# RetNet recurrence and a tanh-shrink layer on one core: a rewritten order of the first eight steps, and the last rows stored in four pieces

## The chip, the core and the metric

The kernel runs on one core of one Trainium2 chip. The metric is device time in microseconds (us), lower is better. A core has TensorE (PE: matrix products, result in PSUM), VectorE (DVE), ScalarE (ACT) and GpSimd (POOL), which each work through their own instructions in order, and SyncE (SP), which here only issues DMAs. They wait for each other through semaphores.

## What is computed

```python
# q, k, v: (4, 8, 768, 64) float32; w_in (512, 2048), w_out (2048, 512) float64
gamma = 1.0 - 2.0 ** (-5.0 - np.arange(H))
for t in range(S):
    state = gamma * state + k_t (outer) v_t        # per batch and head
    y[:, :, t] = (1 / sqrt(D)) * q_t @ state
x = y as (B*S, H*D) = (3072, 512)
h = x @ w_in
out = (h - tanh(h)) @ w_out                        # (3072, 512) float32
```

## The kernel before, in words

The recurrence is done in 24 chunks of 128 tokens (six per batch, `CPB`). A chunk's `q` and `v` are scaled by powers of gamma (`scale`, L241), `k` and `q` are transposed on TensorE (`turn`, L255) and copied to SBUF by ScalarE (`turn_copy`, L267, L269); `products` (L303, L309) makes k-by-v and k-by-q products, `mask` (L316) and `state` (L326 to L332) work on them on VectorE, and `outputs`, `outputs_rest` (L357) accumulate y in PSUM. Between these two, `see` (L387) reads four columns of y. `keep_x` (L402) copies y out as x, transposed.

The layer is done in tiles of 256 tokens (`n`) by 256 hidden columns (`m2`), called steps. `up` (L421) makes h in two halves, `shrink_begin` to `shrink_end` (ScalarE L431 to L449, VectorE L459 to L482) make g = h - tanh(h), `down` (L490) multiplies with w_out and `add_up` (L503) adds up in SBUF. Later steps use a scheme with seven products instead of eight for a pair of 2x2 blocks (`fast_up` L735, `fast_products` L627).

The weights come as float64 and are turned into float32 in the kernel, in blocks of 128 rows or columns: `load_weights` (L154, L159) fetches the raw words, `convert_begin` (ScalarE, L177, L178), `convert_bits` (VectorE, L186 to L192) and `convert_end` (L200, L204, VectorE or GpSimd) build the numbers.

What bears on the order: the program runs with a hand-written schedule (`tc.manual_schedule()`), so each engine and each DMA queue does things in the order in which the Python code names them. For the first eight steps (`BEGUN = 8`) and the first eight chunks that order is a string of pieces, each a letter and a number. The letters: `L` load a chunk's k, q, v; `W` load a weight block; `s`, `w` scale q, v; `t`, `T` transpose k, q; `c`, `C` copy these; `p` products; `m` mask; `z` state; `b`, `r` first and second part of the outputs; `e` see; `y` keep x; `A`, `D`, `G` the three parts of a conversion; `u`, `v` the two halves of an up; `a`, `q`, `d`, `g` the shrink; `o` down; `E` add up; and `x`, which sets how many matmuls on a tile of zeros (`keep_busy`, L217) are put ahead of the next piece of TensorE, in the PSUM place which that piece will write. The numbers count chunks, weight blocks or steps. After this string a loop over the remaining steps sets the order.

Some buffers tie engines together: k and q have two buffers each (`inp`), so chunk c+2 is fetched when the products of chunk c are done; the transposes from chunk 4 on and the products share one pair of PSUM banks (tag `t`); the h banks are two; the last chunks' y share two banks.

At the end (`finish`) the last down products come in four groups, and a chain of additions builds the four quarters c11, c12, c21, c22 of the last 256 rows. `late_c22` copies a PSUM bank on ScalarE (L658) and adds on GpSimd (L659); `store` (L647) writes one of two halves of the rows, 256 KB each.

Of the kernel before, what the change touches and what calls it, by code (L numbers as in the profile page):

```python
# [16 lines left out]
P = 128  # L17
# [7 lines left out]
B0, C0 = 1.1162213056058772, 5.494931718829769  # L25
B1, C1 = -1.609711559785289, 5.546157850574988
# [6 lines left out]
def kernel(  # L33
# [25 lines left out]
    nc = tc.nc  # L59
# [12 lines left out]
    TH = 2 * P  # L72
# [15 lines left out]
    def bank(tag, name):  # L88
        return ps.tile([P, BANK], F32, tag=tag, name=name)
# [25 lines left out]
    w1 = wts.tile([P, NC, DF], F32, name="w1")  # L115
    w2 = wts.tile([P, NM, DM], F32, name="w2")
# [6 lines left out]
    def weight_ends(i):  # L123


        f, r = divmod(i, 2 * NC)
        if r < NC:
            cols = ts(NC * f + r, P)
            rows = w_in[:, cols].rearrange("(k two p) n -> p two k n", two=2, p=P)

            return w1[:, :, cols], [
                (ds(0, P), 0, rows[:, 0]),
                (ds(0, D), 1, rows[D:, 1]),
                (ds(D, D), 1, rows[:D, 1]),
            ]
        m = NC * f + r - NC
        return w2[:, m], w_out[ts(m, P)]
# [57 lines left out]
    def convert_end(i, engine):  # L195
        if i not in words:
            return
        dst, src = weight_ends(i)
        head, low, power = words.pop(i)
        engine.tensor_tensor(low, low, power.bitcast(F32), op=ALU.mult)  # L200
        head = head.bitcast(F32)
        if isinstance(src, list):
            low, head = (t.rearrange("p (c n) -> p c n", c=NC) for t in (low, head))
        engine.tensor_tensor(dst, low, head, op=ALU.add)  # L204
# [10 lines left out]
    def keep_busy(at):  # L215
        for _ in range(idle[0]):
            nc.tensor.matmul(at, busy, busy, start=True, stop=True, skip_group_check=True)  # L217
        idle[0] = 0
# [18 lines left out]
    def scale(ci, which, engine):  # L237
        if ci >= NCH:
            return
        t, g = loaded[ci][1 + which], (gq, gv)[which]  # L240
        engine.tensor_tensor(t, t, g[:, ts(ci % CPB, H)][:, :, None].to_broadcast([P, H, D]),  # L241
                             op=ALU.mult)
# [47 lines left out]
    scores = {}  # L290
# [28 lines left out]
        masked[ci] = m  # L319

    def state(ci):
        halves = scores.pop(ci)
        j = ci % CPB
        if j == 0:
            states[ci] = mid.tile([P, 2, NP, D], F32, tag="state", name=f"state_{ci}", bufs=3)
            nc.vector.tensor_copy(states[ci][:, 1], halves[:, 0, 1])  # L326
        else:
            nc.vector.tensor_tensor(states[ci][:, 1], halves[:, 0, 1], states[ci][:, 0],
                                    op=ALU.add)
        if j < CPB - 1:  # L330
            nxt = mid.tile([P, 2, NP, D], F32, tag="state", name=f"state_{ci + 1}", bufs=3)
            nc.vector.tensor_tensor(nxt[:, 0], halves[:, 1, 1], states[ci][:, 1], op=ALU.add)  # L332
            states[ci + 1] = nxt
# [75 lines left out]
    hps = {}  # L409

    def work(tag, bufs):
        return tmp.tile([P, BANK], F32, tag=tag, name=tag, bufs=bufs)

    def up(n, m2, i):

        if i == 0:
            hps[n, m2] = bank("h", f"h_{n}_{m2}")
        hp = hps[n, m2][:, ts(i, TH)]
        keep_busy(hp[:, :P])
        for c in range(NC):  # L420
            nc.tensor.matmul(hp, w1[:, c, ts(2 * m2 + i, P)], xT[n // 2][:, c, ts(n % 2, TH)],  # L421
                             start=(i == 0 and c == 0), stop=(c == NC - 1),
                             skip_group_check=True)
# [69 lines left out]
    def add_up(n, m2, j):  # L493
        done = 2 * m2 + 2 == NM
        if j == 0 and n not in sums:
            sums[n] = [op.tile([P, 2, DM], F32, tag="sum", name=f"sum_{n}"), set()]
        o, begun = sums[n][0][:, j], sums[n][1]
        if j in begun:
            nc.vector.tensor_tensor(o, o_p[j], o, op=ALU.add)
        elif done and j % 2:  # L500
            nc.vector.tensor_copy(o, o_p[j])
        else:
            nc.scalar.copy(out=o, in_=o_p[j])  # L503
        begun.add(j)
        if done:
            nc.sync.dma_start(out=rows_of(n)[:, j], in_=o)

    def rows_of(n):

        return out[ds(n * TH, TH)].rearrange("(p two) c -> p two c", two=2)  # L510
# [13 lines left out]
    steps = [(n, m2, i == 0, i == len(r) - 1) for r in runs for i, (n, m2) in enumerate(r)]  # L524
# [107 lines left out]
    def sums_of(n):  # L632

        acc = accs[n]
        o = op.tile([P, 2, DM], F32, tag="sum", name=f"sum_{n}")
        c11, c12, c21, c22 = (o[:, j, ts(c, TH)] for j in range(2) for c in range(2))
        some = [mid.tile([P, 2, TH], F32, tag="a", name=f"fast_{n}") for _ in range(2)]
        p1, v_, x_, w_ = (t[:, i] for t in some for i in range(2))

        def add(dst, k, b, sub=False):  # L640
            if sub:
                nc.vector.tensor_tensor(dst, b, acc[k], op=ALU.subtract)
            else:
                nc.vector.tensor_tensor(dst, acc[k], b, op=ALU.add)

        def store(j, queue=nc.sync):
            queue.dma_start(out=rows_of(n)[:, j], in_=o[:, j])  # L647

        todo = {
            "p1": lambda: nc.scalar.copy(out=p1, in_=acc[1]), "c11": lambda: add(c11, 2, p1),  # L650
            "v": lambda: add(v_, 6, p1), "w": lambda: add(w_, 7, v_),
            "c22": lambda: add(c22, 5, w_), "x": lambda: add(x_, 5, v_),
            "c21": lambda: add(c21, 4, w_, True), "c12": lambda: add(c12, 3, x_),
        }

        def late_c22():
            p5 = work("q0", 1)[:, :TH]
            nc.scalar.copy(out=p5, in_=acc[5])  # L658
            nc.gpsimd.tensor_tensor(c22, p5, w_, op=ALU.add)  # L659

        return todo, store, late_c22
# [14 lines left out]
    def finish(n, m2, first, last):  # L676

        todo, store, late_c22 = None, None, None
        for some, then in (((1, 2), ("p1", "c11")), ((6,), ("v",)), ((7, 5), ("w", "x")),
                           ((4, 3), ("c21", "c12"))):  # L680
            fast_products(n, m2, first, last, some)
            if todo is None:
                todo, store, late_c22 = sums_of(n)
            for x in then:
                todo[x]()
                if x == "w":
                    late_c22()
                if x == "c21":
                    store(1, nc.scalar)
        store(0)  # L690

    def end_some(n):
        for _ in range(min(n, len(ending))):
# [85 lines left out]

    BEGUN = 8  # L780
    EARLY_TURNS = 4
    TO_VECTOR = 2

    def tall(ci):
        return nc.vector if ci < TO_VECTOR else nc.gpsimd

    pieces = {
        "L": load_chunk,
        "W": load_weights,
        "s": lambda c: scale(c, 0, tall(c)),  # L790
        "w": lambda c: scale(c, 1, tall(c)),
        "t": lambda c: turn(c, 0, c < EARLY_TURNS),
        "T": lambda c: turn(c, 1, c < EARLY_TURNS),
        "c": lambda c: turn_copy(c, 0),
        "C": lambda c: turn_copy(c, 1 if c < EARLY_TURNS else None),
        "p": products,
        "m": mask,
        "z": state,
        "b": outputs,
        "e": see,  # L800
# [1 line left out]
        "y": keep_x,  # L802
        "A": convert_begin,
        "D": convert_bits,
        "G": lambda i: convert_end(i, tall(i)),
        "u": lambda s: up(*steps[s][:2], 0),
        "v": lambda s: up(*steps[s][:2], 1),
        "a": lambda s: shrink_begin(*steps[s][:2]),
# [2 lines left out]
        "g": lambda s: [f(*steps[s][:2]) for f in (shrink_last_factor, shrink_end)],  # L811
        "o": lambda s: [down(*steps[s][:2], j, *steps[s][2:]) for j in range(2)],
        "E": lambda s: [add_up(*steps[s][:2], j) for j in range(2)],
        "x": lambda n: idle.__setitem__(0, n),
    }
    if w_out.dtype != F32:
        rooms += [xp.tile([P, 2, 2 * BANK], U32, tag="xT", name=f"raws_{i}") for i in range(3)]
    order = """
    L0 x8 t0 c0 s0 x5 T0 w0 L1 C0 x3 t1 W0 p0 c1 s1 m0 x2 T1 z0 W1 C1 w1 x3 b0 p1 e0 A0 r0
    m1 z1 y0 A1 D0 L2 x4 b1 t2 e1 c2 G0 r1 s2 y1 D1 x3 T2 w2 L3 u0 C2 W2 p2 G1 s3 t3 m2 T3  # L820
    w3 c3 v0 z2 C3 b2 A2 L4 p3 e2 W3 D2 a0 r2 s4 y2 w4 q0 W4 m3 z3 G2 x9 t4 b3 A3 d0 T4 e3
    C4 r3 g0 L5 y3 x1 p4 A4 W5 u2 D3 s5 v2 W6 w5 m4 D4 u1 G3 a2 q2 z4 L6 x6 t5 d2 G4 T5 A5
    v1 W7 C5 g2 b4 s6 a1 W8 p5 w6 e4 u3 D5 q1 v3 m5 A6 G5 z5 r4 L7 a3 t6 d1 b5 W9 y4 T6 e5
    o0 s7 g1 C6 w7 A7 W10 D6 q3 r5 t7 W11 T7 D7 G6 y5 C7 x3 u4 d3 v4 G7 A8 g3 p6 a4 o1 A9 m6
    z6 q4 D8 p7 E1 d4 G8 b6 o2 e6 m7 g4 A10 r6 z7 u5 y6 D9 b7 v5 D10 G9 e7 r7 a5 o3 y7 q5
    G10 u6 E3 d5 A11 v6 g5 o4 a6 D11 q6 u7 G11 d6 v7 g6 o5 a7 q7 E5 d7 g7 W12 L8 W13 W14
    """
    for piece in order.split():
        pieces[piece[0]](int(piece[1:]))
# [65 lines left out]
    for s in range(BEGUN, len(steps)):  # L895
        n, m2, first, last = steps[s]
        fast = n >= FAST_UP
        ci = with_chunk.get(s)
# [115 lines left out]
```

## Time and profile before

| what | value |
|---|---|
| median of 7 runs (lowest, highest) | 712.98 us (711.7, 714.05) |
| the profiled execution's own time | 711.87 us |
| its span, first to last instruction | 710.0 us |
| TensorE busy | 698.5 us (98%), zero-tile matmuls included |
| VectorE, ScalarE, GpSimd busy | 576.6, 432.2, 348.1 us |
| DMA | 59.95 MB, mean 84 GB/s |
| zero-tile matmuls ahead of pieces (`x`) | 47, each shown as two records |

A page of the profile gives busy times, the span in 40 equal slices, the chain of work that ended last, the costliest groups and the DMA issues. Other views answer questions: a timeline lists instructions in order of time (start in us, duration in us, engine, line, operation, tiles, shape, count, and in brackets the idle time of that engine before it and what ended it); a table of stages gives each engine's busy time between two times; a list of waits gives who waited for whom. A TensorE float32 matmul appears as two records. In the timeline the duration of the last matmul of a group overlaps the next group by its pipeline depth, so the spacing of starts is what counts.

### The profile page before, as it was taken

What the parts mean: (1) busy time and instruction counts of PE and PEld (TensorE: products, weight loads), DVE (VectorE), ACT (ScalarE), POOL (GpSimd) and SP (SyncE); (2) the same over time, 40 slices, a digit from 0 to 9 for tenths busy, and PEclk for the clock granted to TensorE, in tenths of its full rate; (3) what the DMA queues carried; (4) which work ended last, traced back from release to release, by engine and by line L of the source; (5) the groups of instructions that cost most, each with busy time, mean ns of one, the idle gap of its engine ahead of it and who ended that gap; (6) DMA issues with size and microseconds to landing.
All of it is one profiled execution on the core that took longest, in us unless ns stands there. A gap on an engine that the chain in (4) does not pass through costs nothing.

```text
span 710.0 us, 16725 instructions
## 1 busy us (share of the span) xinstructions
PE 698.5 (98%) x6574; PEld 573.5 (81%) x6574; DVE 576.6 (81%) x976; ACT 432.2 (61%) x814; POOL 348.1 (49%) x493
## 2 busy tenths in 40 slices
PE   8899999999999999999999999999999999999997
PEld 8686666667666776676779999999999999999996
DVE  4999988898899866688687888788787787887885
ACT  4567565777676755566575556666555555665553
POOL 0574436445444582565378854454353544543333
PEclk9999999999999999999999999999999999999999
DMA  9974428966966466555200000000000000000001
GB/s 202 220 198 106 105 61 205 217 172 165 200 186 165 110 161 164 133 150 128 69 32 1 1 2 16 16 1 31 1 1 31 0 1 30 2 16 16 2 16 45
DMA packets 125406, 59.95 MB, mean 84 GB/s; under 512 B 109840, under 2 KB 118160, under 8 KB 125328
## 3 DMA queue, kind: packets, MB, share of 16 engines
q1 hardware_dynamic: 122736, 50.08, 29.6%
q10 hardware_dynamic: 2592, 8.80, 3.2%
q8 instruction: 52, 0.85, 0.5%
q14 instruction: 26, 0.21, 0.1%
HBM read 35.80 MB, written 14.68 MB: 71 GB/s over the span
## 4 chain that ended last, share of the span: by engine, by line
PE 92%; DVE 4%; DMA 1%; ACT 1%; SPq 0%; issue 0%; DVEq 0%; ACTq 0%
PE h L735 28%; PE o L490 18%; PE h L421 15%; PE fast_t L627 9%; PE y L627 8%; PE fast_o L627 7%; PE y L357 3%; PE s L309 1%; PE s L303 1%; PE kqTp L217 1%; PE kqTp L255 1%; DMA raw<-in_moe_w_in_dram 1%; DMA kqT<-rows 1%; DVE head L190 1%; DVE power L192 0%
## 5 line engine op out<-in xcount | busy, mean ns | idle before, releaser
L490 PE MATMUL o<-w,g 128*128 128x512 f32 x320 | 145.9, 594 | 0.0
L434 ACT ACTIVATE th<-h 128x512 f32<-128x512 f32 x64 | 38.2, 597 | 138.8 <-DVE h L752 136.3
L421 PE MATMUL h<-xT,w 128*128 128x256 f32 x512 | 117.8, 382 | 1.4 <-DVE w L204 1.4
L421 PEld LDWEIGHTS h<-xT,w 128*128 128x128 f32 x512 | 95.7, 190 | 21.5 <-issue 7.4
L578 POOL TENSOR_TENSOR s<-g 128x128 f32<-128x128 f32 x56 | 25.6, 457 | 165.3 <-DVE g L482 147.6
L490 PEld LDWEIGHTS o<-w,g 128*128 128x128 f32 x320 | 58.8, 190 | 54.3 <-issue 52.1
L200 POOL TENSOR_TENSOR low<-low,power 128x512 f32<-128x512 f32 x30 | 38.6, 1288 | 102.4 <-DVE power L192 66.5
L735 PEld LDWEIGHTS h<-xT,w 128*128 128x128 f32 x512 | 76.2, 191 | 14.5 <-issue 6.9
L482 DVE COPY_PREDICATED g<-large,th 128x512 f32<-128x512 int32 x96 | 76.7, 799 | 9.8 <-DVE g L481 0.5
L735 PE MATMUL h<-xT,w 128*128 128x128 f32 x512 | 78.7, 276 | 0.2 <-ACT fast_head L740 0.2
L459 DVE TENSOR_TENSOR th<-h,th 128x512 f32<-128x512 f32 x96 | 65.5, 682 | 15.2 <-ACT th L432 13.9
L465 DVE SCALAR_TENSOR_TENSOR h<-q,h 128x512 f32<-128x512 f32 x96 | 66.8, 696 | 11.4 <-ACT q L440 1.5
L750 DVE TENSOR_TENSOR h<-h,fast_head 128x256 f32<-128x256 f32 x64 | 27.6, 432 | 53.8 <-PE h L735 52.0
L440 ACT ACTIVATE q<-u,tab 128x512 f32<-128x512 f32 x96 | 69.7, 726 | 1.7
L448 ACT ACTIVATE q<-u,tab 128x512 f32<-128x512 f32 x96 | 69.5, 723 | 0.0
L745 POOL TENSOR_TENSOR fast_head<-fast_head 128x256 f32<-128x256 f32 x64 | 47.2, 738 | 44.9 <-ACT fast_head L740 33.3
L449 ACT ACTIVATE large<-u,tab 128x512 f32<-128x512 f32 x96 | 68.5, 714 | 0.0
L735 PE MATMUL h<-x,w 128*128 128x128 f32 x448 | 68.3, 275 | 0.0
L460 DVE SCALAR_TENSOR_TENSOR h<-u,h 128x512 f32<-128x512 f32 x96 | 65.9, 687 | 0.0
L735 PEld LDWEIGHTS h<-x,w 128*128 128x128 f32 x448 | 59.0, 192 | 0.0
L740 ACT COPY fast_head<-h 128x512 f32<-128x512 f32 x64 | 37.3, 583 | 24.8 <-PE h L735 24.7
L474 DVE SCALAR_TENSOR_TENSOR g<-q,h 128x512 f32<-128x512 f32 x64 | 44.0, 688 | 7.7 <-ACT q L448 1.1
(192 smaller groups left out, 1465.0 us busy)
## 6 DMA issues: line engine op xcount, KB each, us to landing
rows<-apart ACTq DMA_DIRECT2D x16, 512.0 KB, 4.5
k<-in_k_dram SPq DMA_DIRECT2D x24, 256.0 KB, 4.4
q<-in_q_dram SPq DMA_DIRECT2D x24, 256.0 KB, 5.2
v<-in_v_dram SPq DMA_DIRECT2D x24, 256.0 KB, 5.7
raw<-in_moe_w_out_dram SPq DMA_DIRECT2D x12, 512.0 KB, 4.2
out_dram<-sum SPq DMA_DIRECT2D x23, 256.0 KB, 2.0
raw<-in_moe_w_in_dram SPq DMA_DIRECT2D x14, 256.0 KB, 4.1
raw<-in_moe_w_in_dram SPq DMA_DIRECT2D x28, 128.0 KB, 4.3
```

The source lines that it names most:

```text
L421: nc.tensor.matmul(hp, w1[:, c, ts(2 * m2 + i, P)], xT[n // 2][:, c, ts(n % 2, TH)], start=(i == 0 and c == 0), stop=(c == NC - 1), skip_g ...
L440: nc.scalar.activation(q0, shrinking[n, m2][0], AF.Square, bias=bias0)
L448: nc.scalar.activation(q1, u, AF.Square, bias=bias1, scale=math.sqrt(A))
L449: nc.scalar.activation(large, u, AF.Relu, bias=bias_m)
L459: nc.vector.tensor_tensor(th, hp, th, op=ALU.subtract)
L460: nc.vector.scalar_tensor_tensor(hp, in0=u, scalar=R, in1=hp, op0=ALU.subtract, op1=ALU.mult, reverse0=True)
L465: nc.vector.scalar_tensor_tensor(hp, in0=shrinking[n, m2][2], scalar=C0, in1=hp, op0=ALU.add, op1=ALU.mult)
L482: nc.vector.copy_predicated(flat, large.bitcast(I32), th)
L490: nc.tensor.matmul(o_p[j], gT[n, m2][:, i, ts(j, P)], w2[:, 2 * m2 + i], start=(first and i == 0), stop=(last and i == 1))
L627: nc.tensor.matmul(accs[n][k], left[k - 1], right, start=first and k in (1, 6, 7, 4), stop=last, skip_group_check=True)
L735: nc.tensor.matmul(hps[n, m2][:, ts(PLACE[k], P)], s_of[m2][k - 1][:, c], x_of[n][k - 1][:, c], start=(k == 1 and c == 0), stop=(c == 1), ...
L745: nc.gpsimd.tensor_tensor(odd_room[1], first[:, :2], first[:, 3:1:-1], op=ALU.add)
```

## The change

Three things change. The order string of the first eight steps is another one. In it the zero-tile matmuls are 22 instead of 47, and two of their four places write an h bank, taken early by a new piece `h`. Which engine scales and converts what is now named by sets: VectorE scales q of chunks 2, 4, 5 and v of 0, 1, 2 (before: q and v of 0 and 1); GpSimd scales the others, q of chunks 0 and 1 among them. VectorE still ends the conversion of weight blocks 0 and 1. In `finish`, the store of the last rows goes out in four pieces of 128 KB, each behind the addition that ends its quarter, and `late_c22` comes after the addition `x` instead of ahead of it. `scores.pop` becomes a look-up, so that `z` may stand ahead of `m`. After the string nothing is reordered up to `finish`.

```diff
-        halves = scores.pop(ci)
+        halves = scores[ci]
...
-        if i == 0:
+        if (n, m2) not in hps:
             hps[n, m2] = bank("h", f"h_{n}_{m2}")
...
-        def store(j, queue=nc.sync):
-            queue.dma_start(out=rows_of(n)[:, j], in_=o[:, j])
+        def store(j, some=slice(None), queue=nc.sync):
+            queue.dma_start(out=rows_of(n)[:, j, some], in_=o[:, j, some])
...
+        left, right = (ts(c, TH) for c in range(2))
         for some, then in (((1, 2), ("p1", "c11")), ((6,), ("v",)), ((7, 5), ("w", "x")),
                            ((4, 3), ("c21", "c12"))):
             fast_products(n, m2, first, last, some)
...
             for x in then:
                 todo[x]()
-                if x == "w":
+                if x[0] == "c":
+                    store(int(x[1]) - 1, left if x[2] == "1" else right)
+                if x == "x":
                     late_c22()
-                if x == "c21":
-                    store(1, nc.scalar)
-        store(0)
+        store(1, right, nc.scalar)
...
-    TO_VECTOR = 2
-
-    def tall(ci):
-        return nc.vector if ci < TO_VECTOR else nc.gpsimd
+
+    SCALED = {2, 4, 5}, {0, 1, 2}
+    ENDED = {0, 1}
+
+    def engine(i, among):
+        return nc.vector if i in among else nc.gpsimd
+
+    def begin_h(s):
+
+        hps[steps[s][:2]] = bank("h", "h_early")
+        keep_busy(hps[steps[s][:2]][:, :P])
...
-        "s": lambda c: scale(c, 0, tall(c)),
-        "w": lambda c: scale(c, 1, tall(c)),
+        "s": lambda c: scale(c, 0, engine(c, SCALED[0])),
+        "w": lambda c: scale(c, 1, engine(c, SCALED[1])),
...
-        "G": lambda i: convert_end(i, tall(i)),
+        "G": lambda i: convert_end(i, engine(i, ENDED)),
...
+        "h": begin_h,
...
-    L0 x8 t0 c0 s0 x5 T0 w0 L1 C0 x3 t1 W0 p0 c1 s1 m0 x2 T1 z0 W1 C1 w1 x3 b0 p1 e0 A0 r0
-    m1 z1 y0 A1 D0 L2 x4 b1 t2 e1 c2 G0 r1 s2 y1 D1 x3 T2 w2 L3 u0 C2 W2 p2 G1 s3 t3 m2 T3
-    w3 c3 v0 z2 C3 b2 A2 L4 p3 e2 W3 D2 a0 r2 s4 y2 w4 q0 W4 m3 z3 G2 x9 t4 b3 A3 d0 T4 e3
-    C4 r3 g0 L5 y3 x1 p4 A4 W5 u2 D3 s5 v2 W6 w5 m4 D4 u1 G3 a2 q2 z4 L6 x6 t5 d2 G4 T5 A5
-    v1 W7 C5 g2 b4 s6 a1 W8 p5 w6 e4 u3 D5 q1 v3 m5 A6 G5 z5 r4 L7 a3 t6 d1 b5 W9 y4 T6 e5
-    o0 s7 g1 C6 w7 A7 W10 D6 q3 r5 t7 W11 T7 D7 G6 y5 C7 x3 u4 d3 v4 G7 A8 g3 p6 a4 o1 A9 m6
-    z6 q4 D8 p7 E1 d4 G8 b6 o2 e6 m7 g4 A10 r6 z7 u5 y6 D9 b7 v5 D10 G9 e7 r7 a5 o3 y7 q5
-    G10 u6 E3 d5 A11 v6 g5 o4 a6 D11 q6 u7 G11 d6 v7 g6 o5 a7 q7 E5 d7 g7 W12 L8 W13 W14
+    L0 L1 x8 t0 c0 W0 s0 x4 T0 w0 W1 C0 p0 t1 m0 c1 s1 z0 b0 w1 T1 e0 C1 p1 L2 z1 r0 A0 m1
+    W2 D0 y0 x5 h0 b1 A1 G0 t2 c2 e1 s2 L3 r1 D1 T2 y1 C2 u0 w2 A2 G1 p2 t3 m2 v0 c3 L4 z2
+    s3 W3 D2 T3 w3 a0 b2 C3 e2 q0 r2 p3 d0 G2 y2 L5 m3 W4 w4 z3 A3 x5 h2 b3 W5 s4 t4 D3 e3
+    T4 r3 C4 s5 y3 p4 G3 z4 u2 m4 L6 A4 g0 W6 t5 w5 T5 v2 C5 W7 D4 b4 a2 p5 s6 A5 z5 u1 w6
+    m5 e4 q2 L7 D5 r4 t6 T6 W8 v1 C6 d2 G5 y4 W9 b5 g2 p6 e5 G4 W10 r5 u3 y5 a1 m6 z6 W11 b6
+    s7 A6 v3 D6 q1 t7 o0 d1 G6 A7 e6 a3 g1 w7 A8 r6 T7 u4 C7 D7 y6 q3 p7 z7 G7 v4 m7 d3 b7
+    a4 o1 e7 g3 D8 u5 E1 A9 r7 G8 v5 q4 d4 o2 g4 a5 y7 A10 D9 q5 o3 d5 G9 u6 g5 A11 E3 u7
+    D10 v6 D11 v7 a6 q6 G11 d6 o4 a7 g6 G10 q7 o5 d7 g7 E5 W12 L8 W13 W14
```

## The prediction

> **What bounds the kernel now.** I read the table of stages first, then who TensorE waited for, then each engine's timeline up to 100 us and from 696 us.
>
> From 56 us on TensorE has no gap:
>
> ```profile
> 0.00:13.00 13.00, 11.87 (x175) 11.22 (x179) 4.29 (x8) 3.82 (x7) 0.20 (x4) 1.00 1.05 200
> 13.00:38.00 25.00, 20.07 (x532) 16.82 (x521) 22.80 (x35) 16.02 (x43) 11.26 (x10) 1.00 0.99 226
> 38.00:56.00 18.00, 17.60 (x260) 15.03 (x254) 17.07 (x27) 11.42 (x26) 11.78 (x10) 1.00 0.72 185
> 56.00:84.00 28.00, 28.00 (x336) 17.49 (x335) 26.72 (x41) 18.86 (x46) 13.70 (x12) 1.00 0.39 95
> ...
> 98.00:400.00 302.00, 301.49 (x3185) 217.51 (x3184) 246.12 (x410) 196.00 (x383) 169.12 (x185) 1.00 0.53 135
> 400.00:696.00 296.00, 296.00 (x2021) 278.11 (x2020) 241.48 (x429) 174.10 (x294) 134.45 (x264) 1.00 0.03 12
> ```
>
> The columns are the stretch, its length, busy time of PE, weight load, DVE, ACT and POOL, the granted clock, the DMA share and GB/s. After 98 us TensorE lacks 0.5 us of 598; the kernel is bound by its matmuls and only the beginning and the last microseconds can be shortened. Up to 38 us the DMA engines are full (share 1.0), and TensorE's busy time is partly zero tiles:
>
> ```profile
> 31.26 2.25 PE L217 MATMUL kqTp<-busy 128*128 128x128 f32 x18 [1.82 <-DVE state L332]
> 33.34 0.60 PE L255 MATMUL kqTp<-tab,k 128*128 128x128 f32 x4
> ...
> 36.49 0.49 PE L217 MATMUL s<-busy 128*128 128x128 f32 x2 [0.68 <-ACT kqT L267]
> ...
> 38.00 5.45 PE L421 MATMUL h<-xT,w 128*128 128x256 f32 x24
> 43.85 1.58 PE L217 MATMUL kqTp<-busy 128*128 128x128 f32 x12 [0.40 <-DVE state L332]
> ```
>
> Zero tiles take 3.78 us ahead of the first transpose (needed by nobody before k lands at 4.73) and 10.4 us in ten later places, idle gaps after the start 6.5. The eight steps end at 97.51. VectorE is without a gap of note from 14 us to 93, partly since work beside GpSimd takes longer:
>
> ```profile
> 39.40 1.37 DVE L188 TENSOR_SCALAR head<-head 128x512 uint32<-128x512 uint32 x1
> 40.80 1.65 DVE L190 SCALAR_TENSOR_TENSOR head<-raws,head 128x512 uint32<-128x512 uint32 x1
> ...
> 48.65 0.43 DVE L188 TENSOR_SCALAR head<-head 128x512 uint32<-128x512 uint32 x1
> 49.11 0.69 DVE L190 SCALAR_TENSOR_TENSOR head<-raws,head 128x512 uint32<-128x512 uint32 x1
> ```
>
> At 39.4 GpSimd is converting, at 48.7 it is idle: one `D` takes 4.1 us or 2.0.
>
> **The change, stage by stage.** No useful matmul goes or comes, so I follow the new order through the engines with this trace's durations: t or T 0.43, p 1.09 (0.62 and 0.47), b 0.86 (b0 0.45), r 0.3, half an up 1.75, down 3.44, a zero tile 0.215 (two records of 107 ns); on VectorE a scaling or m 0.6, z 0.85, D 2.0 alone, G 1.4 alone, d and g 2.1 each; on ScalarE A 1.15, c 0.55 (1.0 for two), e 0.45, y 0.6; on GpSimd a scaling 1.05 to 1.2, G 2.6.
>
> 0 to 16 us. The loads of chunks 0 and 1 and weights 0 and 1 keep their order, so q lands at 5.94 and 9.64, v at 7.06 and 10.8, W0 by 13.2. q goes to GpSimd: 5.94+0.15+1.05=7.15, so T0 stands at 7.2 (before: scaled by 6.78, but behind zero tiles until 7.73). p0 waits for v: 7.85 to 8.97. t1 follows with no zero tiles. m0 and the state copy end at 10.05, b0 10.05 (before 12.12); T1 10.85; p1 11.55 to 12.7 (before 12.74 to 13.87). Then y0 stands on ScalarE behind A0, which waits for W0: 13.3+1.15+0.6, so b1 starts at 15.2 (before 16.34). The five zero tiles of h0 lie in that wait and cost nothing.
>
> 16 to 23 us. k2 lands at 16.84 either way; A1 (W1 lands at 16.0), c2, e1, r1, y1 follow, and u0 stands at 19.6 (before 19.90). The gain so far is taken back by the loads. But VectorE does D0, G0, s2, D1, w2, G1 with GpSimd idle: D1 2.1 instead of 3.5, the two G 2.8 instead of 4.3. The second weight block is ready at 22.9 instead of 25.36 in spite of the two scalings put on VectorE (q2 and v2, 1.2).
>
> 23 to 38 us. SP issues W2 ahead of chunk 3: W2 lands at 22.1 (26.1 before), k3 at 23.3, q3 24.5, v3 25.7, each about 2.5 to 3 later. v0 runs at 23.75 (25.42). b2, e2, r2 and p3 wait for q3 and for ScalarE behind a0, so p3 is at 28.15, no gain (28.09). D2, d0, m3, z3 put VectorE at 31.05 for the state that b3 needs; b3 starts at 30.4 and ends at 31.6 (34.7), with h2's zero tiles in the wait ahead of it. s4 on VectorE, T4, then A3 (W3 lands at 31.7), e3 and C4 on ScalarE until 34.3, p4 34.35 (36.91), u2 35.4. In the profile u2 stands at 38.00, with the same work done before it: gain 2.6.
>
> After 38 us. From 38.00 to 97.51 are 59.5 us, of which zero tiles are 2.08 and idle 0.40: 57.0 of work. The new order has no zero tile there. W4 at 37.7 holds A4, and C5 behind it until 39.9, under v2 and b4. u3 wants the h bank that g2 gives back: 0.4 idle; 0.3 more for b6 or t7. So the eight steps end at 35.4+57.0+0.7=93.1: gain 4.4. VectorE is not late: its D's add up to 34.6 before, some 27 in the new order; g1 is done near 58 for o1 at 64, g3 near 67 for u5 at 68, g5 near 80 for o5 at 89.
>
> From step 8 on all is as before. One place has no slack: p8 waited 0.2 us for its transposed k and q (landed 119.01), whose chain starts with the conversions of W12 and W13. They stand behind E5, which waits for the last down. Before, D12 began 2.25 us after the end of the eight steps, behind g7; now g7 is done earlier, and D12 follows A12 at 1.8. So the gain passes.
>
> The tail:
>
> ```profile
> 705.14 0.37 ACT L658 COPY q<-fast_t 128x256 f32<-128x256 f32 x1 [1.44 <-DVE fast L644]
> 705.54 0.42 DVE L644 TENSOR_TENSOR fast<-fast_t,fast 128x256 f32<-128x256 f32 x1 [0.49 <-ACT q L658]
> 705.59 0.72 POOL L659 TENSOR_TENSOR sum<-q,fast 128x256 f32<-128x256 f32 x1 [1.90 <-ACT q L658]
> 705.88 0.41 DVE L642 TENSOR_TENSOR sum<-fast,y 128x256 f32<-128x256 f32 x1
> 706.21 0.42 DVE L644 TENSOR_TENSOR sum<-y,fast 128x256 f32<-128x256 f32 x1
> 706.37 0.34 ACTq L647 DMA_DIRECT2D out_dram<-sum  x1
> 706.65 0.33 SPq L647 DMA_DIRECT2D out_dram<-sum  x1
> ```
>
> The copy holds x back by 0.49. With x first, x runs at 705.0, c21 at 705.5, c12 at 705.85 (0.36 earlier); the copy moves from 705.14 to 705.5, so GpSimd's c22 ends at 706.7 and the last store issues at 706.75, 0.1 later than now, but with 128 KB, while a quarter has left at 704.2. Against the split stands the Trainium skill, SBUF — State Buffer, "The DMA setup-cost knee": a transfer pays about 2 us whatever its size, and is to be as large as can be. The row is 2.0 us to landing for 256 KB. By its fit (2 us plus bytes over 436 GB/s) halving saves 0.3 us of the last landing, an estimate that makes the tail 0.2 shorter; by this run's loading rate (1.2 us per 256 KB) 0.6, making it 0.5. Two stores of 256 KB now overlap, so I take 0.4; the ends are -0.1 and 0.9.
>
> One cost has no row. GpSimd's first tensor operation moves from 18.17 us (the moment its data landed) to about 6, and the program has a reload of GpSimd's library ahead of it, not seen in the trace. The Trainium skill, GPSIMD Engine Reference, "2.1 Instruction dispatch", says that the first call to freshly loaded code pays about 6 us with no instruction visible. If it runs from the start it ends at 6.7 and costs T0 0.8, which the wait for W0 hides (2.2 of slack ahead of b1). If it begins at the call, q is scaled at 13, b1 moves from 15.2 to 19.1 and the loads behind p0 by 2.7: some 3.5 lost of 4.4. The trace only bounds it: ready by 18.17. I take the start, since the reload stands ahead of the wait for data; the other end is in the range.
>
> Sum: 4.4+0.4=4.8. Span 710.0-4.8=705.2, the profiled execution 711.87-4.8=707.1. It lies 1.1 under the median of the runs, so 712.98-4.8=708.2.
>
> **The rivals.** Below, the bound is 0.2% (1.4 us), about what a measurement can tell from no change.
>
> GpSimd starts late (the slower side). If its library is ready only after about 13 us, each further microsecond goes into T0, p0 and so into every load behind p0 and p1; the ready time has no cover there. At 13 the gain is down to about 1; from 14.5 the kernel is slower; at the bound of 18.17, b1 is at 25, some 9.5 late, giving 717. For it: the skill's rule and an operation never tried so early. Against: nothing holds the reload back. 15%; about 715.5. Ready between 8 and 13: 10%, 709.7 to 712.
>
> Loads bind. They are full until 44 us; if W2's earlier place puts W3, L5 and W4 a microsecond or two later than I have them, u2 gains 1 instead of 2.6 and A4's cover goes; or the transposes for p8 follow VectorE and not ScalarE, and p8 waits. Either gives 710 to 711.5; 15%. Against: same bytes, same order up to L2.
>
> Nothing changes: stalls land where zero tiles were, which then were free filling. For it, the zero tiles in the 1.8 us gap at 31 lie in a true wait; against, those at 43.85 and 60.58 do not. 713; 5%.
>
> **How the numbers follow.** My case has 55%, at 708.2 with its own range 706.5 to 709.8 (stalls of 0.3 to 2 instead of 0.7, W3 by a microsecond either way, the tail's ends). With the cases up to 711.9 the range holds about 8 in 10. Faster by over 0.2%: 0.55, most of the 10, nearly all of the 15: 0.76. Slower 0.16, within 0.08.
>
> **What would show it.** Right: b0 near 10, b1 near 15.2, u2 near 35.4, the first step after the string near 93, later starts all 4 to 5 us earlier, p8 without a new wait, D at 2.0 us mostly, last store issued near 702. Wrong: a first GpSimd scaling that starts long after 6 us, a TensorE clock below 1.0 in the gaps, ScalarE waiting for W3 past 32.5, or VectorE releasing TensorE after 50 us.

## The result and the profile after

The changed kernel takes 708.89 us (median of 12 runs, 705.85 to 711.98) against 712.76 us before (31 runs): ratio 0.9947, 95% interval 0.9935 to 0.9958, so 3.9 us or 0.53% faster. The forecast was 708.2 (706.5 to 709.8 for its main case, up to 711.9 with most of its rivals). The profiled execution took 708.68 us, 3.2 less than the one of before, with this span and TensorE time on its page:

```profile
span 706.9 us, 16637 instructions
...
PE 694.0 (98%) x6524; PEld 568.2 (80%) x6524; DVE 568.4 (80%) x978; ACT 431.8 (61%) x814; POOL 344.2 (49%) x491
```

TensorE is still the bound: its busy time fell by 4.5 us. The 25 zero tiles that are gone come to 5.4 us (0.215 each), and a slower clock, shown below, gives some of it back. The table of stages, cut where the new order's stages end (columns as before: stretch, length, busy PE, weight load, DVE, ACT, POOL, clock, DMA share, GB/s):

```profile
13.00:35.00 22.00, 16.44 (x397) 13.23 (x388) 19.68 (x35) 13.88 (x37) 5.78 (x5) 1.00 1.00 212
35.00:53.00 18.00, 17.78 (x375) 15.11 (x376) 14.27 (x26) 10.76 (x28) 11.29 (x9) 0.91 0.93 253
53.00:81.00 28.00, 27.53 (x257) 17.25 (x256) 23.92 (x42) 20.46 (x44) 12.01 (x11) 1.00 0.21 52
81.00:94.00 13.00, 13.00 (x47) 8.74 (x46) 11.19 (x19) 8.09 (x15) 5.44 (x5) 1.00 0.65 150
94.00:400.00 306.00, 305.59 (x3209) 220.82 (x3208) 249.97 (x416) 198.46 (x387) 171.27 (x187) 1.00 0.51 133
```

Two things differ from the table of before. VectorE is no longer full: 14.27 of 18 us from 35 us on, where it had 17.07 of 18. And there is a granted clock of 0.91 in the second row, where the profile of before has 1.00 in every row. (Other executions of the kernel before do lose some clock: in both sets of 22 runs beside the experiments the mean is 0.9983 and the lowest run has 0.995 or 0.997.) TensorE's timeline shows where:

```profile
34.09 0.46 PE L357 MATMUL y<-a,v 64*64 64x64 f32 x16 [1.22 <-ACT seen L387]
35.22 0.69 PE L303 MATMUL s<-v,k 64*64 64x64 f32 x32 [0.67 <-ACT kqT L267]
35.71 0.68 PE L309 MATMUL s<-kqT 64*64 64x64 f32 x32
36.31 3.63 PE L421 MATMUL h_early<-xT,w 128*128 128x256 f32 x8
39.73 0.69 PE L255 MATMUL kqTp<-tab,k 128*128 128x128 f32 x4
40.27 0.60 PE L255 MATMUL kqTp<-tab,q 128*128 128x128 f32 x4
40.70 1.89 PE L421 MATMUL h_early<-xT,w 128*128 128x256 f32 x8
```

u2, the row at 36.31, needs 3.42 us to the next start; v2, the same work at 40.70, needs 1.82. The clock record of this execution has half speed from 36.5 to 39.9 us; below, such a stretch is called a half clock. This one costs 1.6 us. A second one begins at 705.5 us, after the last matmul, and costs nothing; the mean clock of a run counts both.

GpSimd's first tensor operation, the cost that had no row, has one now:

```profile
6.08 1.04 POOL L241 TENSOR_TENSOR q<-q,tab 128x512 f32<-128x512 f32 x1 [5.64 <-DMA q<-in_q_dram]
9.60 1.04 POOL L241 TENSOR_TENSOR q<-q,tab 128x512 f32<-128x512 f32 x1 [2.48 <-DMA q<-in_q_dram]
```

It starts 0.1 us after its data landed (5.94) and takes the 1.04 us of the later ones: no late start, no slow first call. No trace here shows a reload of GpSimd's library, so why it cost nothing stays open.

The tail, with the same operations as shown of before:

```profile
701.54 2.56 SPq L647 DMA_DIRECT2D out_dram<-sum  x3
...
702.82 0.37 ACT L658 COPY q<-fast_t 128x256 f32<-128x256 f32 x1 [1.77 <-DVE fast L644]
702.84 0.42 DVE L642 TENSOR_TENSOR sum<-fast,y 128x256 f32<-128x256 f32 x1
703.18 0.42 DVE L644 TENSOR_TENSOR sum<-y,fast 128x256 f32<-128x256 f32 x1
703.27 0.72 POOL L659 TENSOR_TENSOR sum<-q,fast 128x256 f32<-128x256 f32 x1 [2.23 <-ACT q L658]
704.02 0.34 ACTq L647 DMA_DIRECT2D out_dram<-sum  x1
```

The last row of TensorE, before and then after:

```profile
704.86 0.59 PE L627 MATMUL y<-w,s 128*128 128x256 f32 x2
702.21 0.59 PE L627 MATMUL y<-w,s 128*128 128x256 f32 x2
```

The last matmul ends (start plus duration) at 702.80 here and at 705.45 before. So the last store issues 1.22 us after it, 0.02 later than before (706.65), and the span ends 4.1 us after it instead of 4.6.

### The profile page after: what moved, and what is told of

Read it like the earlier page. It is cut to its first block, busy times and chain, and to the rows that moved or that the text cites. A ratio compares the mean times of both kernels' runs of the same rounds, so it can differ in the third digit from the quotient of the medians.

```text
span 706.9 us, 16637 instructions
## 1 busy us (share of the span) xinstructions
PE 694.0 (98%) x6524; PEld 568.2 (80%) x6524; DVE 568.4 (80%) x978; ACT 431.8 (61%) x814; POOL 344.2 (49%) x491
## 4 chain that ended last, share of the span: by engine, by line
PE 92%; DMA 2%; DVE 2%; ACT 1%; issue 1%; SPq 1%; POOL 0%; POOLq 0%; DVEq 0%; ACTq 0%
PE h L736 28%; PE o L490 19%; PE h L421 15%; PE fast_t L627 8%; PE fast_o L627 7%; PE y L627 7%; PE y L357 3%; PE s L303 1%; PE s L309 1%; PE h_early L421 1%; DMA k<-in_k_dram 1%; DMA v<-in_v_dram 1%; DMA raws<-in_moe_w_in_dram 1%; PE kqTp L255 1%; SPq L234 1%
## 5 line engine op out<-in xcount | busy, mean ns | idle before, releaser
L421 PE MATMUL h<-xT,w 128*128 128x256 f32 x480 | 110.7, 382 | 0.0
L421 PEld LDWEIGHTS h<-xT,w 128*128 128x128 f32 x480 | 89.7, 190 | 19.0 <-issue 7.2
L736 PEld LDWEIGHTS h<-xT,w 128*128 128x128 f32 x512 | 76.2, 191 | 14.5 <-issue 7.2
```

Source lines behind the costliest of these rows:

```text
L736: nc.tensor.matmul(hps[n, m2][:, ts(PLACE[k], P)], s_of[m2][k - 1][:, c], x_of[n][k - 1][:, c], start=(k == 1 and c == 0), stop=(c == 1), ...
```

## The experiments

The theory after the result: the order gives the gain, the tail half a microsecond of it, and most of what is missing from the forecast went to a half clock that TensorE's unfilled waits set off. The rivals: the tail or the division of the scalings carries more than that; or what is missing is the late fourth weight block, on which ScalarE waits. All runs are timed beside runs of the kernel before on the same chip.

**The order alone** (the old `finish` and `store`):

```diff
...
-                if x[0] == "c":
-                    store(int(x[1]) - 1, left if x[2] == "1" else right)
-                if x == "x":
+                if x == "w":
                     late_c22()
-        store(1, right, nc.scalar)
+                if x == "c21":
+                    store(1, nc.scalar)
+        store(0)
```

> The new order with the old end of the kernel. If the gain of 3.9 us is the order's, this run gains 3.4 (3.0 to 4.0) against before and its last matmul starts where the changed kernel's does; if the tail is worth more than its 0.45 of the profiles, it gains under 3.

709.11 us against 712.72; ratio 0.9949 (0.9932 to 0.9966): 3.6 us. From its last matmul's end (702.63) to the end of its span (707.2) are 4.6 us, as before. The order carries the gain. Which of its many moves carry how much was not taken apart.

**The tail alone** (the same edit the other way round, on the kernel before):

> The old order with the new end. By my sum and the two profiles it gains 0.4 to 0.5 us; a rival that the four stores pay their fixed cost four times gives 0 or a loss of a few tenths. It may be too small for the interval, so the time from the last matmul's end to the end of the span is read: 4.55 us before, 4.1 expected.

712.19 us against 712.72; ratio 0.9990 (0.9982 to 0.9999): 0.5 us. From the last matmul's end (706.34) to the end of the span (710.47) are 4.1 us. The four stores do not pay for being four; they land in 1.7 us (SP's three, median) and 1.9 (ScalarE's) at 128 KB. With two stores of 256 KB, ScalarE's took 2.0 (before) and SP's, the last, 2.4 (in the run of the order alone; the trace of before has no landing for it). This run changes the split and the order of the additions together.

**Zero tiles in two waits** (a piece `H` puts them into the h bank that h2 has taken):

```diff
+        "H": lambda s: keep_busy(hps[steps[s][:2]][:, :P]),
...
-    T4 r3 C4 s5 y3 p4 G3 ...
+    T4 x6 H2 r3 C4 s5 y3 x3 H2 p4 G3 ...
```

> The changed kernel with six zero tiles (1.3 us) in TensorE's wait ahead of r3 and three (0.65) in that ahead of p4. Theory: the half clock of 3.4 us at 36.5 us is set off by these waits and costs 1.7; then the granted clock stays at 1.0 until the end and the run is 1 to 1.7 faster than the changed kernel (some 707.5 median). Rival: the half clock comes from elsewhere (the power of the dense stretch, or chance), and the zero tiles change nothing or cost 0 to 0.5.

710.33 us against 712.72; ratio 0.9963 (0.9950 to 0.9976). No gain over the changed kernel. The theory in this form fell: u2 ran at full clock in the profile, but there was a half clock at 18.5 us. Mean granted clock of its runs 0.9957, of the changed kernel's 0.9964, of the kernel before beside it 0.9983.

**No zero tiles after the first stage** (h0 and h2 keep their banks):

```diff
-    ... y0 x5 h0 ... A3 x5 h2 ...
+    ... y0 h0 ... A3 h2 ...
```

> The changed kernel without the zero tiles of h0 and h2 (ten). Theory of the clock: gaps of 2.5 us at 13 to 15.8 and of 1.3 more at 28.7, so one or more half-clock stretches more, each costing up to 1.7: 1 to 4 slower than the changed kernel. Rival, that zero tiles are only filling: no change or 0.1 faster.

710.47 us against 712.72; ratio 0.9969 (0.9958 to 0.9980); mean clock 0.9920. Its profile has half clock from 16.6 to 23.4 and from 37.1 to 40.5. So the ten zero tiles that the change kept are worth about 1.6 us; they are not filling. As a time this is likely, not certain (the interval touches the changed kernel's at 0.9958); the clock is clear, at most 0.993 in each of its seven runs and at least 0.994 in each of the changed kernel's twelve.

These profiles tell what sets the half clock off. Shown are the 3.4 us that stand right before a half clock. The changed kernel, then the half clock itself:

```profile
33.10:36.50 3.40, 1.74 (x81) 1.57 (x82) 2.63 (x6) 2.48 (x9) 1.10 (x1) 1.00 1.02 292
36.50:39.90 3.40, 3.40 (x9) 2.58 (x9) 3.30 (x6) 1.24 (x2) 2.76 (x3) 0.50 0.92 226
```

The kernel with two waits filled:

```profile
15.10:18.50 3.40, 1.56 (x52) 1.21 (x52) 3.16 (x7) 2.50 (x8) 0.00 (x0) 1.00 0.97 192
18.50:21.90 3.40, 2.99 (x24) 2.48 (x25) 3.30 (x7) 1.64 (x9) 0.00 (x0) 0.51 0.91 231
```

The kernel without the ten zero tiles:

```profile
13.20:16.60 3.40, 0.89 (x53) 0.79 (x48) 3.18 (x7) 2.20 (x5) 0.00 (x0) 1.00 1.22 205
33.70:37.10 3.40, 1.02 (x33) 0.67 (x34) 2.18 (x5) 2.92 (x9) 0.06 (x1) 0.99 1.10 225
```

The second number is TensorE's busy time: 1.74, 1.56, 0.89 and 1.02 of 3.40 us. Little work alone is not enough, though. The changed kernel has the place at 15.1 us too, with the same 1.56, and there the clock stayed at 1.00:

```profile
15.10:18.50 3.40, 1.56 (x52) 1.21 (x52) 3.16 (x6) 2.59 (x9) 0.00 (x0) 1.00 0.97 195
18.50:21.90 3.40, 2.98 (x30) 2.19 (x31) 3.30 (x7) 1.43 (x6) 0.00 (x0) 1.00 0.91 215
```

What differs is where the steps of the clock fall. In every profile the times at which the granted clock changes lie whole multiples of 3.413 us apart (changed kernel: 5.78, 36.50 and 39.91; two waits filled: 4.88, 18.54 and 21.95), and this grid starts at another time in each execution. In the changed kernel's profile the grid cuts the place at 15.1 us in two, 12.61 to 16.02 with 2.18 us of work and 16.02 to 19.43 with 2.00. I counted the work in each stretch of the grid, for all ten profiles, up to the stretch in which the last matmul ends. The eight stretches with 1.74 us or less were each followed by a half clock; those at full clock with 1.90 or more never were; between 1.79 and 1.83 both happened. So filling two waits did not drive the half clock elsewhere. The changed kernel has two places that the grid can hit, this run filled one of them, and its profiled execution hit the other.

**Zero tiles in every wait:**

```diff
-    ... y0 x5 h0 ... L3 r1 ... q0 r2 ... x5 h2 b3 ... T4 r3 ... y3 p4 ...
+    ... y0 x10 h0 ... L3 x3 H0 r1 ... q0 x2 h2 r2 ... x5 H2 b3 ... T4 x4 H2 r3 ... y3 x2 H2 p4 ...
```

> The changed kernel with zero tiles in every wait of TensorE between 13 and 36 us (21 more than it has: h0 has ten, and r1, r2, r3 and p4 get three, two, four and two). Theory: the half clock falls on whichever free-running stretch of 3.4 us has had too little work, so only filling all waits keeps the clock: granted clock back to the before kernel's 0.998 and a median 1.5 to 2.5 us under the changed kernel's 708.9. Rival: the clock isn't what costs, and the zero tiles at best change nothing.

707.22 us (706.70 to 708.14) against 712.29; ratio 0.9925 (0.9911 to 0.9938): 5.1 us faster than before, and the fastest version of the study. Mean clock 0.9994, and no half clock within the span of its profile. From 7 to 100 us no stretch of 3.41 us in it, wherever it is laid, has less than 2.30 us of work, so the grid has nothing to hit; in the changed kernel's profile the least is 1.41. The same place of TensorE's timeline:

```profile
33.05 1.06 PE L217 MATMUL h_early<-busy 128*128 128x128 f32 x8
34.19 0.46 PE L357 MATMUL y<-a,v 64*64 64x64 f32 x16
34.58 0.71 PE L217 MATMUL h_early<-busy 128*128 128x128 f32 x4
35.32 0.69 PE L303 MATMUL s<-v,k 64*64 64x64 f32 x32
...
36.41 1.99 PE L421 MATMUL h_early<-xT,w 128*128 128x256 f32 x8
38.24 0.60 PE L255 MATMUL kqTp<-tab,k 128*128 128x128 f32 x4
```

r3, p4 and u2 stand within 0.1 us of where they stood in the changed kernel: there the zero tiles cost 0.1 us at most. u2 now takes 1.83 us. The eight steps end at 92.97 us (the changed kernel: 95.34). Against the changed kernel the two intervals still touch (0.9935 and 0.9938), so the 1.7 us between the medians is likely but not certain as a time; the clock is plain in the records.

**A3 aside** (the conversion that waits on ScalarE for the fourth weight block goes behind the copies for r3 and p4; D3, G3 and A4 go back with it):

```diff
...
-    A3 x5 h2 b3 W5 s4 t4 D3 e3 T4 r3 C4 s5 y3 p4 G3 z4 u2 m4 L6 A4 g0 W6 t5 w5 T5 v2 C5 W7 D4
+    x5 h2 b3 W5 s4 t4 e3 T4 r3 C4 s5 y3 p4 A3 z4 u2 m4 D3 L6 g0 W6 t5 w5 T5 v2 G3 C5 A4 W7 D4
```

> The changed kernel with A3, which waits on ScalarE for the fourth weight block, moved behind the copies that r3 and p4 need, and D3, G3, A4 moved back likewise. If the wait of A3 is what sets u2 late (36.3 instead of my 35.4), u2 stands near 34.8 and the run gains 1 to 1.5 us; if A4 or D3 is then late in their turn, or the clock takes it back, 0 to 0.5.

710.88 us against 712.29; ratio 0.9976 (0.9965 to 0.9987): about 2 us slower than the changed kernel. r3 indeed no longer waits (33.88, with no idle ahead). But VectorE's D4 now runs beside GpSimd, which ends G3 at 43.18 and then scales q and v of a chunk until 45.55:

```profile
41.97 1.50 DVE L186 TENSOR_SCALAR head<-head 128x512 f32<-128x512 f32 x1
43.50 1.15 DVE L188 TENSOR_SCALAR head<-head 128x512 uint32<-128x512 uint32 x1
44.68 1.41 DVE L190 SCALAR_TENSOR_TENSOR head<-raws,head 128x512 uint32<-128x512 uint32 x1
46.13 0.43 DVE L192 TENSOR_SCALAR power<-head 128x512 uint32<-128x512 uint32 x1
46.47 0.42 DVE L328 TENSOR_TENSOR state<-s,state 128x256 f32<-128x256 f32 x1
```

In the changed kernel the same D4 runs with GpSimd idle for most of it:

```profile
39.91 0.42 DVE L186 TENSOR_SCALAR head<-head 128x512 f32<-128x512 f32 x1
40.37 0.43 DVE L188 TENSOR_SCALAR head<-head 128x512 uint32<-128x512 uint32 x1
40.83 0.69 DVE L190 SCALAR_TENSOR_TENSOR head<-raws,head 128x512 uint32<-128x512 uint32 x1
```

D4 takes 4.6 us instead of 2.1. The state behind it begins at 46.47, though p5 was done at 42.78; t6 starts 0.1 us after the mask m5 behind that state has ended (47.49), and a half clock follows (47.5 to 50.9). That t6 waits for the PSUM banks of p5, which the state and m5 read, follows from the kernel; the view names no releaser:

```profile
47.59 1.09 PE L255 MATMUL kqTp<-tab,k 128*128 128x128 f32 x4 [2.27 <-issue]
```

This profile has another half clock, from 20.2 to 23.6, after the place that the changed kernel has at 15 to 19 us.

**Both:**

```diff
-    ... y0 x5 h0 ... L3 r1 ... q0 r2 ... A3 x5 h2 b3 ... D3 e3 ... y3 p4 G3 z4 u2 m4 ...
+    ... y0 x10 h0 ... L3 x3 H0 r1 ... q0 x2 h2 r2 ... x5 H2 b3 ... e3 ... y3 x2 H2 p4 A3 z4 u2 m4 D3 ...
```

> Both: A3 aside and zero tiles in the waits that are left. If both theories hold the gains add: 2.5 to 4 us under the changed kernel, 705 to 706.5, and the clock at 0.998. If only one holds, it equals the better of the two single runs.

709.86 us against 712.29; ratio 0.9958 (0.9945 to 0.9971), clock 0.998. The gains do not add, and it does not equal the better of the two single runs either: it is slower than the one with every wait filled (0.9925), and their intervals lie apart. Its profile shows both sides. u2 starts at 35.05, where it stood at 36.41 with every wait filled and A3 in its old place, so the wait for the fourth weight block is worth 1.4 us at u2. All of that and more is lost at t6, behind a D4 of 4.6 us beside GpSimd:

```profile
35.05 1.99 PE L421 MATMUL h_early<-xT,w 128*128 128x256 f32 x8
...
46.27 0.63 PE L255 MATMUL kqTp<-tab,k 128*128 128x128 f32 x4 [2.24 <-issue]
```

A half clock follows from 47.0 to 50.4. Moving A3 without that collision was not run.

**The old division of the scalings:**

```diff
-    SCALED = {2, 4, 5}, {0, 1, 2}
+    SCALED = {0, 1}, {0, 1}
```

> The new order with the old division of the scalings (VectorE q and v of chunks 0 and 1, GpSimd the rest). My reading is that the order does the work and the sets little: q2 on GpSimd and v2 ahead of G1 with VectorE freed of 0.6, at most 0.5 us to either side. If the division carries the gain (GpSimd beside VectorE slows the conversions), it loses 1 us or more.

707.90 us (705.93 to 711.29) against 712.29; ratio 0.9938 (0.9919 to 0.9956). That is not to be told from the changed kernel's 0.9947. The division carries none of the gain that these runs can tell, and the risk that I saw in it, GpSimd at 6 us, was taken for nothing measurable.

Taken together, the runs of the changed kernel, of the order alone and of the old division (33, the same order of pieces in all three but for the engines and the end) fall apart by their clock: median 706.7 us for the ten with a mean granted clock of 0.998 or more, 709.1 for the other 23. Over all 33 the clock goes with about half of the spread (r squared 0.55), over the changed kernel's twelve alone with less (0.23); what makes the rest is not known.

## Why the prediction was right, and which terms were off

The bound. Right: only the start and the end moved. From the first step after the string to the last matmul's end are 607.9 us before (97.51 to 705.45) and 607.5 after (95.34 to 702.80). The ten profiles have 607.4 to 608.7 there, so these 0.5 us are not told from chance.

0 to 35 us. The followed starts held to 0.6 us: T0 7.17 (forecast 7.2), b0 10.35 (10.05), b1 15.77 (15.2), u0 19.96 (19.6), v0 23.47 (23.75), p3 27.66 (28.15), b3 30.02 (30.4). The conversions on VectorE took 2.1 us with GpSimd idle, as said. The 6.5 us of idle gaps "after the start" include the 1.05 us ahead of the first matmul; this did not enter the sum.

u2. 36.31 instead of 35.4: W3's words were on ScalarE at 32.48, not 31.7. Its last piece was issued at 27.5 and took 4.9 us; I had laid the loads end to end instead of from their issue. So the gain up to u2 was 1.7 us where the forecast had 2.6. In the run of both, with that wait out of the way, u2 starts at 35.05.

After u2. Here is the term that failed. I counted the zero tiles as time to be saved (2.08 us) and the waits as harmless, and named a clock below 1.0 only as a sign of being wrong. 59.0 us went by from u2 to the end of the eight steps where I had 57.7: the work was 57.0 as summed, the waits 0.5 (inside b6) where I had allowed 0.7, and the half clock took 1.6, for which I had put nothing. So the steps ended at 95.34 and not at 93.1: in the profiled execution the start gained 2.2 us of the 4.4 forecast, and the later starts are 2.2 to 2.7 us earlier where I had said 4 to 5. In the run with all waits filled the same stretch is 56.6 us and the steps end at 92.97. That this meets my 93.1 is in part luck, since u2 stands 1.0 later there than forecast and the stretch behind it is 1.1 shorter.

The tail. 0.5 by the profiles and by the run of the tail alone, 0.4 forecast. The last landing is what got shorter, not the last issue.

p8. No new wait; even the 0.2 us of before are gone, as the chain argument had it.

The rivals. GpSimd starting late did not come: it was ready by 6.08 us. "Loads bind" was right as to W3, which put u2 0.9 us later. "Stalls land where zero tiles were, which then were free filling" was close to the truth, but I gave it the wrong price: zero tiles in these waits are not free filling, they keep the clock (0.9920 without the last ten, 0.9994 with every wait filled). The rule for it stands in the Trainium skill, TensorE: Matmul & The Clock Gate, "Why this matters for your kernels": no idle gaps over some 3 us. By its letter the changed kernel was safe, since its longest gap in the place is 1.22 us. Here the measurement decides: the sum over 3.4 us counts, and 1.74 us of work in 3.40 was too little.

The sum. 4.8 forecast; 3.9 measured between the medians, 3.2 between the two profiled executions. The 3.2 are the 4.8 less 0.9 (W3) and 1.6 (half clock), and plus 0.2 (fewer waits), 0.1 (tail) and the 0.5 of the middle that nobody forecast, with 0.1 of rounding. So the mechanism, the order followed through the queues, was right. That the sum came so near owes something to the extra 0.5, and to the half clock not costing as much in every execution.

## What to carry to other kernels

Follow the new order through every engine's queue with the old trace's durations; that put this change's starts up to 35 us within 0.6 us. Before crediting the removal of filler matmuls, add up TensorE's busy time over stretches of 3.4 us, wherever they may be laid: where it falls to about half, the clock can drop, and fillers placed inside true waits cost next to nothing (0.1 us here) and save up to 1.7 us for each half clock they prevent. Fill all such places, since one that is left can still be hit. Put a conversion on VectorE where GpSimd has nothing to do, and check what a moved piece then runs beside: here this cost more than the wait that the move removed.

## What the runs showed of the hardware

The half clock needs no idle gap of its own length: 1.74 and 1.56 us of work in 3.40 were enough, with no single gap over 1.4 us, and it comes in pieces of 3.4 us (6.8 once). In the run with all waits filled, stretches at the same places with 2.69 and 3.29 us of work kept the clock:

```profile
15.10:18.50 3.40, 2.69 (x63) 2.26 (x61) 3.16 (x7) 2.62 (x7) 0.00 (x0) 1.00 0.88 174
33.10:36.50 3.40, 3.29 (x95) 2.80 (x93) 2.58 (x5) 2.58 (x9) 0.99 (x1) 1.00 1.11 317
```

The limit lies nearer to the lower figure. On the clock's own grid of 3.41 us, up to the last matmuls, the kernel before kept full clock after 1.79 us of work (27.65 to 31.06) and the run with A3 aside after 1.90 (13.37 to 16.78), while the run of the order alone lost it after 1.80 (32.92 to 36.33) and the run with A3 aside after 1.82 (16.78 to 20.19). One stretch that the last matmuls end in kept it with 1.59 (702.37 to 705.78, in the run of both), so the profile's busy time tells only roughly when the clock drops. As the grid starts elsewhere in each execution, executions of one program can differ in which places are hit; the mean clocks of the changed kernel's twelve runs go from 0.994 to 1.000. Their times lie up to 6 us apart, and this is one cause of it, not the only one.
